# Three rounds between a split and its output products: a re-timed software pipeline on one TensorE

## Chip, cores and metric

The kernel runs on one NeuronCore of a Trainium2 chip. The metric is the device time of one execution in microseconds (us). PE is TensorE (matmuls), PEld its weight loads, DVE VectorE, ACT ScalarE, POOL GpSimd, SP the engine whose queue issues the DMAs.

## What is computed

```python
X = np.fft.fft(np.fft.fft(x, axis=1), axis=2).real     # x is (8, 3072, 256)
x = X.reshape(8 * 3072, 256)
h = x @ w_in                                           # (256, 2048)
x = (h - np.tanh(h)) @ w_out                           # (2048, 256)
h = x @ w_in2                                          # (256, 1024)
sm = softmax(h); solu = h * sm
ln = (solu - mean(solu)) / sqrt(var(solu) + 1e-6) * g_ln
out = ln @ w_out2                                      # (1024, 256)
```

All of it is float32. The kernel keeps the accuracy by writing each float32 operand as a high and a low part and adding the products high x high, high x low, low x high (`PASSES`).

## The kernel before, in words

A first stage of some 190 us makes the Fourier transform with the symmetry of a real input, so that only half of the columns are computed, and converts the weights. What follows, about 3450 us, is one loop over **rounds** (`step` in the code, 768 of them): 48 groups `n` of 512 tokens, 16 blocks `m` of 128 hidden units. In a round TensorE makes the hidden block `h` (line 879: `parity` for the block before, then `even` for this one, six products of 256 columns), then adds an older block's share to the 512 tokens' second-layer input `x2p` (`o1`, line 941, six products of 512 columns). VectorE combines the block (`act_in`, line 904), subtracts the tanh (`act_out`, line 921) and prepares the next block (`lead`, line 897); ScalarE takes the tanh (line 912) and the high part of the result; GpSimd takes the low part (line 169, called from `rest`). For two of eight blocks VectorE takes the low part instead (`low_by_vector`).

The second layer (`layer2`) is laid over these rounds in a fixed order written by hand. Two tiles of 128 tokens make a **pair**; a pair comes every eight rounds, and each of its works stands at so many rounds behind the pair's start ("back" in the lists `ahead`, `early` and `late`, which say where in a round the work is put into the engines' queues: before the loop's own VectorE preparation, before `o1`, or after it). I count the eight rounds of the cycle from 0 to 7, so that back 17 is position 1. Each engine works through its own queue in order; a semaphore holds an instruction until what it reads is written and what it overwrites has been read.

For a pair, `product` (line 970) makes seven products with the second hidden matrix in two PSUM banks, `bank_a` and `bank_b` (Strassen's scheme in Winograd's form: the first product also goes, by a ScalarE copy, line 1114, into the other bank; `kept`, line 985, copies a finished half out, `block`, line 992, combines halves on VectorE and takes the maximum). Then come the exponential (`power`, ScalarE), the weighing with it (`weigh`, VectorE, line 1016), the square sum (`square`), three small GpSimd steps for the norm (`scale`), and the transposition (`turn`): VectorE transposes 32x32 blocks (line 1046), one DMA writes them to DRAM and four read them back into `um`, with the tokens moved to the free dimension (line 1052). `split_moved` takes the high part of half a tile on ScalarE and the low part on GpSimd, into `ut`, a ring of two buffers. `outp` multiplies each half with the last weights: four times a product of 512 columns with the high part (line 1074) and one of 256 columns with the low part (line 1081), all into one tile `po`. `scaled` brings `po` out: ScalarE scales one half into `o` (line 1092), VectorE adds the other (line 1093), SP stores it.

Before, the cycle's second half reads: splits at backs 14, 16, 18, 20; output products at 15, 17, 19, 21; `scaled` at 18 and 22, in the list ahead of everything else that VectorE does for the second layer. There is one PSUM bank for `po`, `p_t`, with one buffer: a tile's first output product waits until the tile before it is scaled and added. The other seven banks hold `x2p` (two), `bank_a`, `bank_b` and `h` (three).

Of the kernel before, what the change touches and what calls it, by code (L numbers as in the profile page):

```python
# [10 lines left out]
F32 = mybir.dt.float32  # L11
# [3 lines left out]
AF = mybir.ActivationFunctionType  # L15
ALU = mybir.AluOpType
# [4 lines left out]
B, S, D = 8, 3072, 256  # L21
FF1, FF2 = 2048, 1024
P = 128
# [116 lines left out]
def fft2_moe_moe_kernel(  # L140
    ctx: ExitStack, tc: tile.TileContext, xr, x8, xn, xn8, w_in, w_out, w_in2, w_out2, g_ln, tt, t8, ft, out
):
    nc = tc.nc
# [556 lines left out]
    for q in range(NQ):  # L700
# [28 lines left out]
        if q == NQ - 4:  # L729
            nc.sync.dma_start(out=wnu, in_=wnu_d.rearrange("o (m p) -> p (o m)", p=P))  # L730
            nc.sync.dma_start(
                out=nu_h, in_=nu_d[:, PAIRS : PAIRS + 1].rearrange("b o -> o b").to_broadcast([P, B])
# [22 lines left out]
    wk = pool(ctx, "wk", 2, side="left")  # L755
# [15 lines left out]
    B11, B21, B22, T1, T2, T3, T4 = range(7)  # L771
# [3 lines left out]
    A11, A12, A21, A22, S1, S4, S2, S3 = range(8)  # L775
# [92 lines left out]
    bank_a = p_pr.tile([P, HF], F32, tag="a", name="bank_a")  # L868
# [96 lines left out]
    h2s, es, us, sts, uts, pts, pos, o2s, moved = {}, {}, {}, {}, {}, {}, {}, {}, {}  # L965

    def product(p, bank, a, b, start=False):

        for q, (hx, hw) in enumerate(PASSES):
            nc.tensor.matmul(  # L970
                in_pairs(bank),
                xs[:, hx, xs_at[a]],
                in_turn(wi2[:, b, hw]),
                start=(start and q == 0),
                stop=(q == 2),
                skip_group_check=True,
            )

    def new_u(t):
        us[t] = (wk.tile([P, FF2], F32, tag="u", bufs=3, name=f"u{t}"), None)  # L980
        sts[t] = wk.tile([P, 12], F32, tag="st", bufs=8, name=f"st{t}")
        return us[t][0]

    def kept(t, f):
        nc.scalar.copy(out=us[t][0][:, f * HF : (f + 1) * HF], in_=bank_b)
# [3 lines left out]
    def block(t, f, bank, other, first):  # L989

        u, st = us[t][0][:, f * HF : (f + 1) * HF], sts[t]
        nc.vector.tensor_tensor_reduce(  # L992
            out=u,
            in0=bank,
            in1=u if other else nothing_more.to_broadcast([P, HF]),
            scale=-1.0,
            scalar=FLOOR if first else st[:, 7:8],
            op0=ALU.add,
            op1=ALU.min,
            accum_out=st[:, 7:8] if first else st[:, 0:1],  # L1000
        )
# [20 lines left out]
    def square(t):  # L1022

        u, e = us[t]
        st = sts[t]
        nc.scalar.activation(out=st[:, 3:4], in_=st[:, 2:3], func=AF.Copy, scale=-1.0 / (32 * FF2))
        nc.scalar.activation(  # L1027
            out=e, in_=u, func=AF.Square, scale=1.0 / 32, bias=st[:, 3:4], accum_out=st[:, 6:7]
        )

    def scale(t):

        st = sts[t]
        g = nc.gpsimd
        g.tensor_scalar(
            out=st[:, 4:5], in0=st[:, 1:2], scalar1=1e-9, scalar2=1e-3, op0=ALU.add, op1=ALU.mult
        )
        g.tensor_scalar(  # L1038
            out=st[:, 5:6], in0=st[:, 4:5], scalar1=st[:, 4:5], scalar2=st[:, 6:7], op0=ALU.mult, op1=ALU.add
        )  # L1040
        g.tensor_tensor(out=st[:, 10:11], in0=st[:, 5:6], in1=mhalf, op=ALU.pow)  # L1041

    def turn(t):
        u = us[t][0]
        tb = mv.tile([P, FF2], F32, tag="t", bufs=1, name=f"tb{t}")
        nc.vector.transpose(out=tb, in_=u)  # L1046
        d = mv_d[t % len(mv_d)]
        nc.sync.dma_start(out=d, in_=tb)
        m = mv.tile([P, FF2], F32, tag="m", name=f"um{t}")
        blocks = d.rearrange("(q p) (k a j) -> a p k q j", q=4, a=4, j=32)  # L1050
        for a in range(4):
            nc.sync.dma_start(
                out=m[32 * a : 32 * a + 32].rearrange("p (k q j) -> p k q j", q=4, j=32), in_=blocks[a]
            )
        moved[t] = m

    def split_moved(t, half):
        m = moved[t][:, half * 512 : (half + 1) * 512]
        ut = wk.tile([P, 2, 512], F32R, tag="ut", bufs=2, name=f"ut{t}_{half}")
        rnd(ut[:, 0], m)  # L1060
        rest(nc.gpsimd, ut[:, 1], m, ut[:, 0])
        uts[t, half] = ut
        if half:
            moved.pop(t)

    def outp(t, half):
        if half == 0:
            pos[t] = taken(bank_o, [P, 512], "t", f"po{t}")
        po = pos[t]
        ut = uts.pop((t, half))  # L1070
        for k4 in range(4):
            k = half * 4 + k4
            ks = slice(k4 * P, (k4 + 1) * P)
            nc.tensor.matmul(  # L1074
                in_pairs(po),
                ut[:, 0, ks],
                wo2[:, k].rearrange("p h x n -> p (x n) h"),
                start=(k == 0),
                stop=False,
            )  # L1080
            nc.tensor.matmul(  # L1081
                in_pairs(po[:, :D]),
                ut[:, 1, ks],
                wo2[:, k, :, 0].rearrange("p h n -> p n h"),
                start=False,
                stop=(k == NK2 - 1),
            )

    def scaled(t):
        po, by = pos.pop(t), sts.pop(t)[:, 10:11]  # L1090
        o = wk.tile([P, D], F32, tag="o", bufs=3, name=f"o{t}")
        nc.scalar.activation(out=o, in_=po[:, D:], func=AF.Copy, scale=by)  # L1092
        nc.vector.scalar_tensor_tensor(
            out=o, in0=po[:, :D], scalar=by, in1=o, op0=ALU.mult, op1=ALU.add
        )
        us.pop(t)
        nc.sync.dma_start(out=out[t * P : (t + 1) * P, :], in_=o)
# [8 lines left out]
    def layer2(step, place):  # L1106

        works = {
            "ahead": (
                (0, lambda p: product(p, bank_a, A11, B11, True)),  # L1110
                (2, lambda p: product(p, bank_a, A12, B21)),
                (4, lambda p: product(p, bank_b, S3, T3)),
                (6, lambda p: product(p, bank_b, A22, T4)),
                (1, lambda p: nc.scalar.copy(out=bank_b, in_=bank_a)),
                (3, lambda p: (new_u(2 * p), kept(2 * p, 1))),
                (5, lambda p: (new_u(2 * p + 1), kept(2 * p + 1, 1))),
            ),
            "early": (
                (15, lambda p: outp(2 * p + 1, 0)),
                (17, lambda p: outp(2 * p + 1, 1)),  # L1120
                (19, lambda p: outp(2 * p, 0)),
                (21, lambda p: outp(2 * p, 1)),
                (18, lambda p: scaled(2 * p + 1)),
                (22, lambda p: scaled(2 * p)),
                (3, lambda p: block(2 * p, 0, bank_a, False, True)),
                (5, lambda p: block(2 * p + 1, 1, bank_a, True, True)),
                (6, lambda p: block(2 * p + 1, 0, bank_b, False, False)),
                (7, lambda p: block(2 * p, 1, bank_a, True, False)),
                (7, lambda p: power(2 * p + 1)),
                (8, lambda p: (power(2 * p), weigh(2 * p + 1))),  # L1130
                (9, lambda p: weigh(2 * p)),
                (10, lambda p: (square(2 * p + 1), scale(2 * p + 1), turn(2 * p + 1))),
                (12, lambda p: (square(2 * p), scale(2 * p), turn(2 * p))),
                (14, lambda p: split_moved(2 * p + 1, 0)),
                (16, lambda p: split_moved(2 * p + 1, 1)),
                (18, lambda p: split_moved(2 * p, 0)),
                (20, lambda p: split_moved(2 * p, 1)),
                (-1, lambda p: split_x2(p, A11, A12)),
                (1, lambda p: split_x2(p, S2, S3)),
                (3, lambda p: split_x2(p, A22, S4)),  # L1140
            ),
            "late": (
                (2, lambda p: product(p, bank_b, S2, T2)),
                (4, lambda p: product(p, bank_a, S1, T1, True)),
                (6, lambda p: product(p, bank_a, S4, B22)),
            ),
        }
        for back, work in works[place]:
            p = pair_at(step, back)
            if p is not None:  # L1150
                work(p)
# [92 lines left out]


    base = 4 * NG - 8
    block(base + 2, 1, bank_a, True, False)
    first.close()
    p_o = pool(ctx, "p_o", 2, space=PSUM)
    p_h2 = pool(ctx, "p_h2", 2, space=PSUM)  # L1250
# [77 lines left out]
    def exponent(t):  # L1328
        power(t, h2s.get(t))

    def weighed(t):
        weigh(t, h2s.pop(t, None))

    works = {
        "T": trans, "r": high, "l": low_of, "H": h2, "W": outp, "w": last_outp, "X": x_high, "x": x_low,
        "m": peak, "e": exponent, "u": weighed, "q": square, "c": scale, "o": scaled, "M": split_moved,
        "z": last_store,
    }
    todo = """X4 x4 e3 W10 M11 X5 H40 x5 e2 M00 u3 W11 o1 M01 H41 W00 m4 T30 e4 u2 W01 o0 r30 H50 T31 l30 X6 r31 q3 c3 x6
# [55 lines left out]
```

## Time and profile before

| | |
|---|---|
| runs | 3709.53, 3725.9, 3733.6 us; median 3725.9 |
| profiled execution | 3713.57 us, span 3711.8 us from first to last instruction |
| busy share | TensorE 84%, weight loads 70%, VectorE 62%, ScalarE 55%, GpSimd 53% |
| clock of TensorE granted on the mean | 0.913 of 2.4 GHz |

A matmul's busy time is modelled and overlaps with its neighbour's, so the distance between the starts of two groups of matmuls is the better measure. "Idle before" and the waits name what released the instruction. A half granted clock (0.5) is 1.2 GHz.

### The profile page before, as it was taken

How to read it: one execution, taken by the hardware profiler on the slowest of the kernel's cores; microseconds unless marked ns; L12 is line 12 of the kernel's file. 1: busy time of each engine (PE TensorE's matmuls, PEld its weight loads, DVE VectorE, ACT ScalarE, POOL GpSimd, SP SyncE). 2: the span in 40 equal slices, each digit the busy share in tenths (PEclk: the TensorE clock that was granted, in tenths of full speed). 3: DMA queues.
4: the chain of work that ended last, by engine and by line, in shares of the span. 5: the costliest groups of instructions: out<-in, count | busy, mean ns of one | idle time of the engine just before them, and what ended most of it. 6: DMA issues, size and time to landing. Idle time of an engine off the chain costs nothing.

```text
span 3711.8 us, 47081 instructions
## 1 busy us (share of the span) xinstructions
PE 3107.8 (84%) x15073; PEld 2607.3 (70%) x15073; DVE 2300.3 (62%) x4577; ACT 2046.2 (55%) x3990; POOL 1966.5 (53%) x2121
## 2 busy tenths in 40 slices
PE   9998888888888888888888888888888888888888
PEld 5777677776677767776777677767776776677766
DVE  9975665556656565656566665565565566656665
ACT  4565555555555555555555555555555555555555
POOL 0275555555555555555555555555555555555553
PEclk9999998889888998988999988998898999889999
DMA  9813232323232323232333322332232323232322
GB/s 359 304 39 72 64 77 69 69 67 74 63 74 62 77 66 74 69 73 66 72 69 73 74 63 69 73 74 63 69 73 66 71 68 73 67 70 69 73 64 53
DMA packets 882648, 302.96 MB, mean 82 GB/s; under 512 B 788544, under 2 KB 844144, under 8 KB 879104
## 3 DMA queue, kind: packets, MB, share of 16 engines
q1 hardware_dynamic: 879792, 293.45, 31.9%
q10 hardware_dynamic: 2304, 6.42, 0.4%
q8 instruction: 120, 1.97, 0.2%
q14 instruction: 128, 1.05, 0.1%
q0 software_dynamic: 304, 0.07, 0.0%
HBM read 161.26 MB, written 138.60 MB: 81 GB/s over the span
## 4 chain that ended last, share of the span: by engine, by line
PE 39%; POOL 18%; ACT 15%; issue 12%; DVE 11%; DMA 3%; SPq 1%; ACTq 0%; POOLq 0%; DVEq 0%
PE x2p L941 17%; POOL ut L169 10%; PE po L1074 9%; PE po L1081 7%; PE h L879 5%; ACT t L912 5%; DVE h L904 4%; POOL gh L169 4%; ACT gh L166 4%; ACT e L1027 4%; ACT o L1092 2%; DMA um<-mv_d 2%; DVE u L992 2%; POOL st L1038 2%; POOL st L1041 2%
## 5 line engine op out<-in xcount | busy, mean ns | idle before, releaser
L169 POOL TENSOR_TENSOR gh<-t,gh 128x512 fp32r<-128x512 f32 x584 | 877.1, 1502 | 898.4 <-ACT gh L166 536.1
L941 PE MATMUL x2p<-gh,wo 128*128 128x512 f32 x4608 | 1304.3, 426 | 0.0
L912 ACT ACTIVATE t<-h 128x512 f32<-128x512 f32 x762 | 454.3, 596 | 1535.5 <-DVE h L904 1252.2
L941 PEld LDWEIGHTS x2p<-gh,wo 128*128 128x128 f32 x4608 | 977.0, 220 | 166.4 <-POOL gh L169 0.4
L904 DVE SCALAR_TENSOR_TENSOR h<-asb,h 128x256 f32<-128x256 f32 x762 | 322.5, 423 | 1169.1 <-PE h L879 1168.0
L1081 PE MATMUL po<-wo,ut 128*128 128x256 f32 x1528 | 518.1, 339 | 403.6 <-POOL ut L169 403.6
L169 POOL TENSOR_TENSOR ut<-um,ut 128x512 fp32r<-128x512 f32 x372 | 506.4, 1361 | 536.9 <-ACT ut L166 536.9
L1074 PE MATMUL po<-wo,ut 128*128 128x512 f32 x1528 | 671.0, 461 | 107.4 <-ACT ut L166 97.3
L879 PEld LDWEIGHTS h<-zs,wt 128*128 128x128 f32 x4572 | 656.7, 196 | 141.0 <-PE h L879 84.1
L879 PE MATMUL h<-zs,wt 128*128 128x256 f32 x4572 | 667.7, 279 | 72.9 <-DVE gh L169 70.6
L1081 PEld LDWEIGHTS po<-wo,ut 128*128 128x128 f32 x1528 | 343.9, 225 | 486.2 <-POOL ut L169 486.1
L1074 PEld LDWEIGHTS po<-wo,ut 128*128 128x128 f32 x1528 | 332.2, 217 | 197.2 <-ACT ut L166 159.4
L921 DVE TENSOR_TENSOR t<-h,t 128x512 f32<-128x512 f32 x578 | 394.6, 683 | 0.0
L166 ACT ACTIVATE gh<-t 128x512 fp32r<-128x512 f32 x584 | 367.8, 630 | 3.4 <-DVE t L921 1.9
L897 DVE SCALAR_TENSOR_TENSOR asb<-nb,wnu,h 128x256 f32<-128x256 f32 x762 | 358.6, 471 | 0.0
L1016 DVE SCALAR_TENSOR_TENSOR u<-u,e 128x1024 f32<-128x1024 f32 x188 | 330.0, 1755 | 0.0
L970 PE MATMUL bank_a<-wi,xs 128*128 128x512 f32 x1128 | 306.3, 380 | 2.4 <-POOL xs L169 1.5
L169 POOL TENSOR_TENSOR xs<-xb,xs 128x256 fp32r<-128x256 f32 (+1 forms) x282 | 231.6, 821 | 57.7 <-ACT xs L166 53.7
L1046 DVE STREAM_TRANSPOSE tb<-u 128x1024 f32<-128x1024 f32 x186 | 230.0, 1237 | 0.0
L970 PE MATMUL bank_b<-wi,xs 128*128 128x512 f32 x846 | 229.7, 380 | 0.2 <-POOL xs L169 0.2
L166 ACT ACTIVATE ut<-um 128x512 fp32r<-128x512 f32 x372 | 229.8, 618 | 0.0
L1027 ACT ACTIVATE e<-u,st 128x1024 f32<-128x1024 f32 x192 | 221.5, 1154 | 6.2
(156 smaller groups left out, 3018.1 us busy)
## 6 DMA issues: line engine op xcount, KB each, us to landing
mv_d<-tb SPq DMA_DIRECT2D x186, 512.0 KB, 2.6
um<-mv_d SPq DMA_DIRECT2D x744, 128.0 KB, 3.7
out<-o SPq DMA_DIRECT2D x192, 128.0 KB, 1.7
x<-xr SPq DMA_DIRECT2D x23, 1024.0 KB, 10.8
zf<-z_d SPq DMA_DIRECT2D x64, 128.0 KB, 2.5
z_d<-zt ACTq DMA_DIRECT2D x16, 392.0 KB, 6.5
wi<-w_in SPq DMA_DIRECT2D x6, 1024.0 KB, 9.4
z_d<-zt SPq DMA_DIRECT2D x16, 384.0 KB, 10.1
```

What stands on the lines that cost most here:

```text
L166: nc.scalar.activation(out=o, in_=i, func=AF.Copy)
L169: eng.tensor_tensor(out=o, in0=i, in1=hi.bitcast(F32), op=ALU.subtract)
L879: nc.tensor.matmul(in_pairs(hs[n, m][:, 0]), wt[c][:, hw, u, o : o + P], in_turn(zs[:, hz, u]), start=(u == 0 and i == 0), stop=(i == 2), ...
L897: nc.vector.scalar_tensor_tensor(out=asb, in0=zg[n][1], scalar=wnu[:, m : m + 1], in1=hs[n, m][:, 0], op0=ALU.mult, op1=ALU.add)
L904: nc.vector.scalar_tensor_tensor(out=h[:, 1], in0=as_.pop((n, m)), scalar=2.0, in1=h[:, 0], op0=ALU.mult, op1=ALU.subtract)
L912: nc.scalar.activation(out=t, in_=h, func=AF.Tanh)
L921: nc.vector.tensor_tensor(out=g, in0=h, in1=t, op=ALU.subtract)
L941: nc.tensor.matmul(in_pairs(x2p[n][mt]), wo1[c][:, hw, k, mt * P : (mt + 1) * P], in_turn(gh[:, hg]), start=(m == 0 and i == 0), stop=(m = ...
L970: nc.tensor.matmul(in_pairs(bank), xs[:, hx, xs_at[a]], in_turn(wi2[:, b, hw]), start=(start and q == 0), stop=(q == 2), skip_group_check= ...
L1027: nc.scalar.activation(out=e, in_=u, func=AF.Square, scale=1.0 / 32, bias=st[:, 3:4], accum_out=st[:, 6:7])
L1074: nc.tensor.matmul(in_pairs(po), ut[:, 0, ks], wo2[:, k].rearrange("p h x n -> p (x n) h"), start=(k == 0), stop=False,)
L1081: nc.tensor.matmul(in_pairs(po[:, :D]), ut[:, 1, ks], wo2[:, k, :, 0].rearrange("p h n -> p n h"), start=False, stop=(k == NK2 - 1),)
```

## The change

Output products stand three rounds behind their split (backs 17, 19, 21, 23 for splits at 14, 16, 18, 20). `scaled` keeps only ScalarE's part, put at the end of the rounds of the second halves (backs 19 and 23); VectorE's addition and the store become `store`, a round later (20 and 24), and stand in the list behind `weigh` and `turn`. The first product of a pair, A11 x B11, moves from the front of position 0 to its end, behind `o1`. The copy of a half for the pair's second tile (`new_u`, `kept` for `2p + 1`, in the title U3's copy) moves from the front of position 5 to the end of position 4. One output half that falls behind the last round, and its `scaled` and `store`, are added after the loop.

```diff
     def scaled(t):
-        po, by = pos.pop(t), sts.pop(t)[:, 10:11]
-        o = wk.tile([P, D], F32, tag="o", bufs=3, name=f"o{t}")
-        nc.scalar.activation(out=o, in_=po[:, D:], func=AF.Copy, scale=by)
+        o = o2s[t] = wk.tile([P, D], F32, tag="o", bufs=3, name=f"o{t}")
+        nc.scalar.activation(out=o, in_=pos[t][:, D:], func=AF.Copy, scale=sts[t][:, 10:11])
+
+    def store(t):
+        o = o2s.pop(t)
         nc.vector.scalar_tensor_tensor(
-            out=o, in0=po[:, :D], scalar=by, in1=o, op0=ALU.mult, op1=ALU.add
+            out=o, in0=pos.pop(t)[:, :D], scalar=sts.pop(t)[:, 10:11], in1=o, op0=ALU.mult, op1=ALU.add
         )
         us.pop(t)
         nc.sync.dma_start(out=out[t * P : (t + 1) * P, :], in_=o)
...
             "ahead": (
-                (0, lambda p: product(p, bank_a, A11, B11, True)),
...
-                (5, lambda p: (new_u(2 * p + 1), kept(2 * p + 1, 1))),
             ),
             "early": (
-                (15, lambda p: outp(2 * p + 1, 0)),
-                (17, lambda p: outp(2 * p + 1, 1)),
-                (19, lambda p: outp(2 * p, 0)),
-                (21, lambda p: outp(2 * p, 1)),
-                (18, lambda p: scaled(2 * p + 1)),
-                (22, lambda p: scaled(2 * p)),
+                (17, lambda p: outp(2 * p + 1, 0)),
+                (19, lambda p: outp(2 * p + 1, 1)),
+                (21, lambda p: outp(2 * p, 0)),
+                (23, lambda p: outp(2 * p, 1)),
...
                 (12, lambda p: (square(2 * p), scale(2 * p), turn(2 * p))),
+                (20, lambda p: store(2 * p + 1)),
+                (24, lambda p: store(2 * p)),
...
             "late": (
+                (0, lambda p: product(p, bank_a, A11, B11, True)),
                 (2, lambda p: product(p, bank_b, S2, T2)),
                 (4, lambda p: product(p, bank_a, S1, T1, True)),
                 (6, lambda p: product(p, bank_a, S4, B22)),
+                (4, lambda p: (new_u(2 * p + 1), kept(2 * p + 1, 1))),
+                (19, lambda p: scaled(2 * p + 1)),
+                (23, lambda p: scaled(2 * p)),
             ),
...
     base = 4 * NG - 8
+    outp(base - 2, 1)
     block(base + 2, 1, bank_a, True, False)
+    scaled(base - 2)
+    store(base - 2)
```

## Rows read from the trace of the kernel before

**Rows 1.** Page, part 1: busy us (share of the span) xinstructions by engine

```profile
PE 3107.8 (84%) x15073; PEld 2607.3 (70%) x15073; DVE 2300.3 (62%) x4577; ACT 2046.2 (55%) x3990; POOL 1966.5 (53%) x2121
```

**Rows 2.** Waits, whole span: engine line <- releaser: us, times, longest

```profile
PEld po L1081 <- POOL ut L169: 486.1, 278, 1.9
...
PEld po L1074 <- ACT ut L166: 159.4, 276, 1.5
...
PEld h L879 <- PE h L879: 84.1, 91, 1.1
...
DVE u L992 <- ACT u L985: 74.8, 94, 1.9
```

**Rows 3.** Timeline of TensorE, positions 7, 0, 1, 2, 3: start, us, instruction

```profile
1816.14 0.57 PE L879 MATMUL h<-zs,wt 128*128 128x256 f32 x3 [0.74 <-DVE gh L169]
1816.55 0.38 PE L1074 MATMUL po<-wo,ut 128*128 128x512 f32 x1
...
1817.86 1.46 PE L941 MATMUL x2p<-gh,wo 128*128 128x512 f32 x6
1819.15 0.83 PE L879 MATMUL h<-zs,wt 128*128 128x256 f32 x6
1819.82 0.81 PE L970 MATMUL bank_a<-wi,xs 128*128 128x512 f32 x3
1820.47 1.46 PE L941 MATMUL x2p<-gh,wo 128*128 128x512 f32 x6
1821.77 0.83 PE L879 MATMUL h<-zs,wt 128*128 128x256 f32 x6
1823.08 0.48 PE L1074 MATMUL po<-wo,ut 128*128 128x512 f32 x1 [0.48 <-ACT ut L166]
1825.16 0.38 PE L1081 MATMUL po<-wo,ut 128*128 128x256 f32 x1 [1.60 <-POOL ut L169]
...
1827.66 0.83 PE L879 MATMUL h<-zs,wt 128*128 128x256 f32 x6
...
1830.92 0.83 PE L879 MATMUL h<-zs,wt 128*128 128x256 f32 x6
```

**Rows 4.** Cores: span and granted clock on the mean

```profile
core 0: 3711.8 us, clock 0.913
```

**Rows 5.** One line over the span: min/median/max ns, first and last start

```profile
L1016 DVE SCALAR_TENSOR_TENSOR u<-u,e x188: 1209/1619/2314, 234.1 to 3670.3; 128x1024 f32<-128x1024 f32 x188
```

**Rows 6.** Windows: length, busy (instructions) PE, PEld, DVE, ACT, POOL, clock, DMA, GB/s

```profile
1825.16:1830.92 5.76, 5.75 (x32) 5.20 (x32) 3.70 (x9) 3.44 (x8) 3.85 (x3) 1.00 0.00 0
...
1834.05:1838.22 4.17, 4.17 (x14) 3.46 (x15) 0.37 (x1) 0.31 (x1) 2.47 (x5) 0.59 0.42 68
1811.64:1886.06 74.42, 62.10 (x314) 53.01 (x313) 45.77 (x91) 42.45 (x83) 40.77 (x44) 0.93 0.32 73
```

**Rows 7.** Timeline of VectorE, positions 0 to 2 of the cycle of rows 3

```profile
1821.68 2.30 DVE L1016 SCALAR_TENSOR_TENSOR u<-u,e 128x1024 f32<-128x1024 f32 x1
...
1823.92 0.42 DVE L904 SCALAR_TENSOR_TENSOR h<-asb,h 128x256 f32<-128x256 f32 x1
...
1828.19 0.43 DVE L904 SCALAR_TENSOR_TENSOR h<-asb,h 128x256 f32<-128x256 f32 x1 [1.39 <-PE h L879]
```

**Rows 8.** Timeline of VectorE, position 0 of the next cycle

```profile
1856.71 0.43 DVE L904 SCALAR_TENSOR_TENSOR h<-asb,h 128x256 f32<-128x256 f32 x1 [1.71 <-PE h L879]
...
1858.04 1.37 DVE L1016 SCALAR_TENSOR_TENSOR u<-u,e 128x1024 f32<-128x1024 f32 x1
```

**Rows 9.** VectorE's output addition over the span

```profile
L1093 DVE SCALAR_TENSOR_TENSOR o<-po,st,o x191: 483/484/486, 270.8 to 3707.4; 128x256 f32<-128x256 f32 x191
```

**Rows 10.** Timeline of GpSimd, position 0 of the cycle of rows 3

```profile
1821.51 1.40 POOL L169 TENSOR_TENSOR gh<-t,gh 128x512 fp32r<-128x512 f32 x1 [1.60 <-issue]
```

**Rows 11.** Reads of the transposed tile: landing, from issue

```profile
DMA to landing us min/median/max: 2.8/3.7/5.1
```

**Rows 12.** Timeline of SP after the transposition of position 2

```profile
1831.94 0.32 SPq L1048 DMA_DIRECT2D mv_d<-tb  x1
1834.90 3.77 SPq L1052 DMA_DIRECT2D um<-mv_d  x4
```

More of the change, by code (lines that the diff above doesn't have):

```diff
@@ L1329, in exponent, with stored @@
         power(t, h2s.get(t))
+    def stored(t):
+        scaled(t)
+        store(t)
     def weighed(t):
@@ L1335, in fft2_moe_moe_kernel @@
         "T": trans, "r": high, "l": low_of, "H": h2, "W": outp, "w": last_outp, "X": x_high, "x": x_low,
-        "m": peak, "e": exponent, "u": weighed, "q": square, "c": scale, "o": scaled, "M": split_moved,
+        "m": peak, "e": exponent, "u": weighed, "q": square, "c": scale, "o": stored, "M": split_moved,
         "z": last_store,
```

## The prediction

> **What bounds the kernel now.** The page comes first: TensorE is the fullest engine, VectorE, ScalarE and GpSimd are between 53 and 62% busy [rows 1]. So the question is what TensorE waits for. The list of waits answers it: its weight loads stood 486.1 us for GpSimd's low part of `ut`, 159.4 us for ScalarE's high part of it, and 84.1 us at `h` [rows 2]. The first two are the output products, which stand one round behind their split. The timeline of TensorE then shows where: in an odd round the first output product waits 0.48 us for the high part, the next 1.60 us for the low part [rows 3], while the even rounds run without a gap.
>
> From the same timeline comes what a pair costs TensorE without waits at full clock [rows 3]: six products of `h` take 0.67 us (1819.15 to 1819.82), a product of the second layer 0.65 (to 1820.47), `o1` 1.30 (to 1821.77), four output products of each kind 1.31 (1816.55 to 1817.86). Position 0 is 2.62 us, positions 2, 4, 6 are 3.26 (1827.66 to 1830.92), an odd position 0.67 + 1.31 + 1.30 = 3.28. The cycle of eight: 2.62 + 3 x 3.26 + 4 x 3.28 = **25.5 us**.
>
> What it takes now: the 188 `weigh` start between 234.1 and 3670.3 us [rows 5], which is 93 cycles and one round of some 4 us, so **36.9 us** a cycle (two cycles in one window: 74.42 [rows 6]). The difference is accounted for. Output products run in about 92 cycles; (486.1 + 159.4 + 84.1)/92 = 7.9 us are waits. The granted clock of 0.913 [rows 4] means 8.7% of the span's work lost, 323 us or 3.5 us a cycle. 25.5 + 7.9 + 3.5 = 36.9. The clock falls behind those waits: from 1825 to 1831 it was 1.00 with TensorE busy throughout, from 1834 to 1838, right after another wait for a split, 0.59 [rows 6], between the levels 2.4 and 1.2 GHz. So nothing but these waits and the clock stands between 36.9 and 25.5; the most that can be gained is 11.4 x 92 = 1049 us.
>
> **The change, part by part.** *Output products three rounds later.* The low part is ready about 1.6 us after TensorE wants it in the next round [rows 3]; two further rounds of over 3 us put it some 5 us ahead. This removes 486.1 + 159.4 us, 7.0 a cycle. The work itself stays the same. The ring of `ut` has two buffers, so ScalarE's split of position 2 now waits for the output products of position 1, one round back instead of three: ScalarE comes to it some 3.5 us into its round, the products end before that round begins. No cost; if the cover were gone, ScalarE's queue (the next tanh) would stand behind it.
>
> *`scaled` split in two.* VectorE no longer stands in positions 2 and 6 for ScalarE's half, and the addition (0.48 us [rows 9]) leaves position 6. There it had delayed the low part behind it, for which TensorE stood 0.74 us in position 7 [rows 3], 84.1 us in all. I let that go to zero: without the addition the low part ends about 3.2 us into a round of 3.26, and TensorE needs it 0.33 later.
>
> *The bank of `po`: the new wait.* The next tile's first output product may start only when the addition has read the one bank. In position 4 the addition ends 0.53 + 1.33 + 1.24 (transposition) + 0.48 = 3.6 us after the round's start, TensorE wants the bank at 3.26 + 0.67 = 3.9: covered by 0.3 us. In position 0 it is not, for the addition stands behind `weigh`. VectorE's first step follows TensorE's round by 0.53 us (1827.66 to 1828.19 [rows 3, 7]). In one cycle `weigh` starts 2.53 us into the round and the next instruction could start at 4.77 (1823.92 - 1819.15 [rows 3, 7]); with the addition 5.25. TensorE wants the bank at 2.62 + 0.67 = 3.29: it waits **2.0 us**. In the next cycle, where no sum of the second layer's inputs lies ahead of it, `weigh` starts 1.86 us into the round (1858.04 less 1856.71, plus 0.53) and ends at 3.2 [rows 8]: with the addition 3.7, a wait of **0.4 us**; there the copy for the next group moves closer in ScalarE's and GpSimd's queue, so I take 0.8. Both cycles alternate. Behind the added wait of TensorE stands its whole queue, `o1` and the next `h`, and behind the later VectorE its `act_in` of position 1.
>
> *First product to the end of position 0.* Same work, 0.65 us; the copy of position 1 stands behind ScalarE's tanh, which needs a later product of TensorE anyway, so it costs nothing. `o1` comes 0.65 us earlier in that round; GpSimd's low part of the block is used by its last two products, 0.9 us after the first, so it stays covered. *U3's copy to position 4.* ScalarE has it half a round earlier, and VectorE's wait of 74.8 us [rows 2] goes; off the path, nothing gained. ScalarE's positions 4 and 3 get 0.6 and 0.5 us fuller, 3.7 and 2.7 of 3.3.
>
> *SP.* The stores move behind the five DMAs of a transposition; `o` has three buffers, so the next writer comes a cycle and a half later. The transposed tile is the tighter one. Position 2's transposition ends 3.1 us into its round, the write takes 3.0 until SP goes on to the reads and these 3.8 to issue [rows 12], and a read lands 2.8 to 5.1 us after its issue [rows 11]: 12.7 to 15.0 us. ScalarE splits it in position 6, at 13.0 + 2.1 = 15.1. Covered, by 0.1 at worst; before, with longer rounds, by far more.
>
> *Other engines.* Two cycles hold 45.8 us of VectorE, 42.5 of ScalarE, 40.8 of GpSimd [rows 6]: 22.9, 21.2 and 20.4 in a cycle of 27 to 28. None becomes the bound by its sum, but VectorE is at 83%.
>
> *The clock.* The trace of before shows no long wait that stands alone, so I bound it. Now 3.5 us a cycle are lost behind three waits of about 2 us (positions 1, 3 and 5; the 0.74 us of position 7 are followed by full clock), 1.2 us each. A lone wait of 2.0 us costs between 0 and that; I take 1.2, since it is the same wait at the same place, and 0 in the cycle with 0.8 us.
>
> **The sum.** One cycle 25.5 + 2.0 + 1.2 = 28.7, the next 25.5 + 0.8 = 26.3, mean **27.5**. 36.9 - 27.5 = 9.4 us, in 92 cycles 865 us. The loop's end gets eight matmuls and one addition outside, some 2 us. 3713.6 - 865 + 2 = **2850 us**, against a profiled execution that lies 0.3% under the median of the runs shown (3725.9); I keep 2850.
>
> **Rivals.** *A, GpSimd first everywhere.* `weigh` took 1209 to 2314 ns [rows 5]. In the long case GpSimd had begun a low part 0.17 us before it and took 1.40 us [rows 7, 10], so VectorE stood about 1.1 us; in the short case `weigh` was first. With rounds shifted against each other GpSimd may be first in every position 0: a wait of 1.5 to 2.0 us in both cycles, with the lower clock behind both: 25.5 + 1.9 + 1.2 = 28.6 and over, 92 x 1.1 = 100 us more, 2950. For it: GpSimd's copy work moves closer to that place. Against it: the order was the same in all cycles of before.
> The Trainium skill (SBUF — State Buffer, section "SBUF: two separate sides") has a rule for this pair: a VectorE instruction with two SBUF inputs and a GpSimd instruction lock a shared pair of ports, whoever starts first holds it to its end and the other blocks. The durations above agree with it, and by it the output addition, with one input in PSUM, isn't held, as its 483 to 486 ns show [rows 9].
>
> *B, the in-order queues.* Long odd rounds let the three other engines catch up; without them a small lateness can come back to TensorE, as at position 7 now (0.74 us), or a late transposed tile can hold ScalarE's split and the tanh behind it. If four of eight rounds lost 0.74, the cycle would be 30.5 us, 3125; all eight, 33.4 and 3390. Against: I followed each engine's queue through a cycle of 27.5 us, and found no other wait; for: margins of 0.1 to 0.5 us.
>
> *C, the bank's ring makes it slower.* One bank goes from first product to addition twice in a cycle. Now that takes three rounds of four, then all four. If ScalarE's half or the addition slipped behind two further rounds at each tile, the ring would be 6 rounds, the cycle 12 rounds of 3.26, 39.1 us: 92 x 2.2 = 200 us slower, 3915. It decides from 18.5 us a ring (37/2); the rows give 12.4 to 14.5.
>
> *D, it doesn't do what it says:* if the output products still waited for a split (a late tile read), 36 to 37 us a cycle, within 1% of before.
>
> **How the numbers follow.** Forecast (2770 to 2920): 0.65. A (2920 to 2990): 0.12. B (2990 to 3450): 0.13. Better than 2770 (no loss of clock, short waits): 0.05. D 0.02, C 0.03. The range of 8 in 10 takes the forecast, A and the near part of B: 2770 to 3060. A per cent is about what a measurement here can tell from none. Faster by over 1%: 0.95; within 1%: 0.02; slower: 0.03.
>
> **What would show it.** Right: the waits for `ut` gone from TensorE; in their place waits of the first output product for VectorE's addition, about 92, half of them near 2 us; rounds of 2.6 to 3.3 us elsewhere; a granted clock of 0.97 or more; VectorE over 75% busy. Wrong: TensorE waiting for `gh`, `h` or `xs` in many rounds, ScalarE idle at `ut` for the read, or a clock still near 0.91 with shorter waits.

## The result, and the profile after

The changed kernel takes **2815.0 us** (median of four runs, 2809.4 to 2820.3) where the kernel before takes 3725.6: a ratio of **0.756**, 95% interval 0.753 to 0.7589. The forecast was 2850, with 2770 to 3060. The profiled execution took 2820.3 us.

Part 1 of the page after, and its chain of work that ended last (share of the span by engine):

```profile
PE 2698.5 (96%) x15073; PEld 2380.6 (84%) x15073; DVE 2258.5 (80%) x4577; ACT 2029.2 (72%) x3990; POOL 1980.9 (70%) x2121
...
PE 82%; DVE 11%; issue 4%; DMA 1%; ACT 1%; POOL 0%; SPq 0%; DVEq 0%; POOLq 0%; ACTq 0%
```

The busy time of the three other engines is what it was to within 2% [rows 1], in a span 24% shorter; TensorE's fell by 13% for the same instructions, since fewer of them run at half clock. The chain ends on TensorE, with VectorE as the only other engine of weight. The granted clock and `weigh` over the span:

```profile
core 0: 2818.5 us, clock 0.984
```

```profile
L1016 DVE SCALAR_TENSOR_TENSOR u<-u,e x188: 1209/1291/2347, 241.5 to 2777.0; 128x1024 f32<-128x1024 f32 x188
```

From the first to the last `weigh` it is 93 cycles and a round of some 4 us, as before [rows 5]: (2777.0 - 241.5 - 4)/93 = **27.2 us** a cycle, 27.5 were forecast, 36.9 it had been. Between the first and the last `weigh` that saves 901 us (3436.2 to 2535.5); the first one starts 7 us later than before, and 893 us are left, by which the profiled executions differ.

The waits of TensorE after, of the whole list, which has the first stage in it too, those over 8 us:

```profile
PEld po L1074 <- DVE o L1095: 113.3, 94, 2.2
...
PEld x2p L941 <- POOL gh L169: 15.0, 51, 1.0
...
PEld h L879 <- DVE asb L897: 8.4, 12, 2.4
```

The two waits for `ut` and the one at `h` [rows 2] are gone, 730 us; one has come, 94 times, for VectorE's addition into `o` (now line 1095), that is, for the one bank of `po`. Cycles come in two kinds by turns: in a long one two sums of the second layer's inputs (line 957) lie ahead of `weigh` in position 0, in a short one they do not. The timeline of TensorE shows where the wait is; positions 7, 0, 1 and 2 of a long cycle (start, us, instruction):

```profile
1518.16 1.46 PE L941 MATMUL x2p<-gh,wo 128*128 128x512 f32 x6
1519.46 0.83 PE L879 MATMUL h<-zs,wt 128*128 128x256 f32 x6
1520.12 1.46 PE L941 MATMUL x2p<-gh,wo 128*128 128x512 f32 x6
1521.42 0.81 PE L970 MATMUL bank_a<-wi,xs 128*128 128x512 f32 x3
1522.07 0.83 PE L879 MATMUL h<-zs,wt 128*128 128x256 f32 x6
1524.75 0.48 PE L1074 MATMUL po<-wo,ut 128*128 128x512 f32 x1 [1.85 <-DVE o L1095]
...
1526.16 1.46 PE L941 MATMUL x2p<-gh,wo 128*128 128x512 f32 x6
1527.46 0.83 PE L879 MATMUL h<-zs,wt 128*128 128x256 f32 x6
```

Position 7 no longer has its gap [rows 3]. In position 1 the first output product starts 2.68 us into the round (1522.07 to 1524.75) where 0.67 would do: 2.0 us. VectorE in the same place:

```profile
1521.32 0.75 DVE L957 TENSOR_TENSOR xb<-xb 128x256 f32<-128x256 f32 x2
1521.99 2.30 DVE L1016 SCALAR_TENSOR_TENSOR u<-u,e 128x1024 f32<-128x1024 f32 x1
...
1524.22 0.47 DVE L1095 SCALAR_TENSOR_TENSOR o<-po,st,o 128x256 f32<-128x256 f32 x1
1524.62 0.41 DVE L904 SCALAR_TENSOR_TENSOR h<-asb,h 128x256 f32<-128x256 f32 x1
```

and GpSimd, whose low part starts 0.18 us before `weigh`:

```profile
1521.81 1.40 POOL L169 TENSOR_TENSOR gh<-t,gh 128x512 fp32r<-128x512 f32 x1 [1.09 <-PE x2p L941]
```

`weigh` takes 2.30 us behind it, as it did before [rows 7, 10], and the addition stands behind `weigh`. The rounds of position 1 in four long cycles one after the other, as windows (length, busy by engine, granted clock, DMA), and the wait in the second of them:

```profile
1412.92:1418.31 5.39, 3.54 (x21) 3.08 (x20) 5.39 (x10) 3.31 (x7) 4.25 (x3) 1.00 0.07 24
1466.57:1473.64 7.07, 5.22 (x22) 4.32 (x21) 5.42 (x10) 3.31 (x7) 5.92 (x4) 0.76 0.05 19
1522.07:1527.46 5.39, 3.54 (x21) 3.08 (x20) 5.39 (x10) 3.31 (x7) 4.25 (x3) 1.00 0.07 24
1575.72:1582.80 7.08, 5.23 (x22) 4.32 (x21) 5.43 (x10) 3.32 (x7) 5.94 (x4) 0.76 0.06 20
```

```profile
1469.25 0.48 PE L1074 MATMUL po<-wo,ut 128*128 128x512 f32 x1 [1.85 <-DVE o L1095]
```

The wait is the same in all four. In the second and the fourth the clock then falls, and the round takes 1.7 us longer. Over the whole trace the clock falls behind 21 of the 44 waits of some 2 us, and behind none of the shorter ones: 21 x 1.7 = 36 us. So the new wait costs twice, the second time in about half of the long cycles.

### The profile page after: what moved, and what is told of

It is laid out like the page before. It is cut to its first block, busy times and chain, and to the rows that moved or that the text cites. A ratio compares the mean times of both kernels' runs of the same rounds, so it can differ in the third digit from the quotient of the medians.

```text
span 2818.5 us, 47312 instructions
## 1 busy us (share of the span) xinstructions
PE 2698.5 (96%) x15073; PEld 2380.6 (84%) x15073; DVE 2258.5 (80%) x4577; ACT 2029.2 (72%) x3990; POOL 1980.9 (70%) x2121
## 4 chain that ended last, share of the span: by engine, by line
PE 82%; DVE 11%; issue 4%; DMA 1%; ACT 1%; POOL 0%; SPq 0%; DVEq 0%; POOLq 0%; ACTq 0%
PE x2p L941 31%; PE h L879 15%; PE po L1074 13%; PE bank_b L970 7%; PE bank_a L970 6%; PE po L1081 6%; DVE u L1016 4%; DVE asb L897 2%; PE pz L486 1%; DVE h L904 1%; DVE o L1095 1%; PE pz L505 1%; DVE xb L957 1%; DVE t L921 1%; PE pw L397 1%
## 5 line engine op out<-in xcount | busy, mean ns | idle before, releaser
L941 PE MATMUL x2p<-gh,wo 128*128 128x512 f32 x4608 | 1148.8, 386 | 1.4 <-POOL gh L169 1.4
L169 POOL TENSOR_TENSOR gh<-t,gh 128x512 fp32r<-128x512 f32 x584 | 809.3, 1386 | 383.7 <-ACT gh L166 257.5
L941 PEld LDWEIGHTS x2p<-gh,wo 128*128 128x128 f32 x4608 | 846.2, 193 | 126.3 <-POOL gh L169 15.0
L169 POOL TENSOR_TENSOR ut<-um,ut 128x512 fp32r<-128x512 f32 x372 | 546.3, 1469 | 182.4 <-PE x2p L941 136.0
L879 PE MATMUL h<-zs,wt 128*128 128x256 f32 x4572 | 638.4, 276 | 6.0 <-DVE asb L897 4.7
L1074 PE MATMUL po<-wo,ut 128*128 128x512 f32 x1528 | 546.9, 397 | 95.8 <-DVE o L1095 94.8
L1081 PE MATMUL po<-wo,ut 128*128 128x256 f32 x1528 | 425.6, 279 | 0.0
L1074 PEld LDWEIGHTS po<-wo,ut 128*128 128x128 f32 x1528 | 295.4, 193 | 146.8 <-DVE o L1095 113.3
L1081 PEld LDWEIGHTS po<-wo,ut 128*128 128x128 f32 x1528 | 300.0, 196 | 0.2
L1016 DVE SCALAR_TENSOR_TENSOR u<-u,e 128x1024 f32<-128x1024 f32 x188 | 295.7, 1573 | 0.0
L970 PEld LDWEIGHTS bank_a<-wi,xs 128*128 128x128 f32 x1128 | 206.2, 189 | 25.4 <-POOL xs L169 0.2
```

The costliest lines, as they stand in the source:

```text
L169: eng.tensor_tensor(out=o, in0=i, in1=hi.bitcast(F32), op=ALU.subtract)
L879: nc.tensor.matmul(in_pairs(hs[n, m][:, 0]), wt[c][:, hw, u, o : o + P], in_turn(zs[:, hz, u]), start=(u == 0 and i == 0), stop=(i == 2), ...
L941: nc.tensor.matmul(in_pairs(x2p[n][mt]), wo1[c][:, hw, k, mt * P : (mt + 1) * P], in_turn(gh[:, hg]), start=(m == 0 and i == 0), stop=(m = ...
L970: nc.tensor.matmul(in_pairs(bank), xs[:, hx, xs_at[a]], in_turn(wi2[:, b, hw]), start=(start and q == 0), stop=(q == 2), skip_group_check= ...
L1016: nc.vector.scalar_tensor_tensor(out=u, in0=u if h is None else h, scalar=-1.0 if h is None else 1.0, in1=e, op0=ALU.mult, op1=ALU.mult, a ...
L1074: nc.tensor.matmul(in_pairs(po), ut[:, 0, ks], wo2[:, k].rearrange("p h x n -> p (x n) h"), start=(k == 0), stop=False,)
```

## The experiments

Each kernel is the changed one with the edit shown, unless it says otherwise. All were run in groups beside the kernel before (medians 3721 to 3727 us). The cycle times are from the first and last `weigh`, as above.

**One round again.**

```diff
-                (17, lambda p: outp(2 * p + 1, 0)),
-                (19, lambda p: outp(2 * p + 1, 1)),
-                (21, lambda p: outp(2 * p, 0)),
-                (23, lambda p: outp(2 * p, 1)),
+                (15, lambda p: outp(2 * p + 1, 0)),
+                (17, lambda p: outp(2 * p + 1, 1)),
+                (19, lambda p: outp(2 * p, 0)),
+                (21, lambda p: outp(2 * p, 1)),
...
-                (20, lambda p: store(2 * p + 1)),
-                (24, lambda p: store(2 * p)),
+                (18, lambda p: store(2 * p + 1)),
+                (22, lambda p: store(2 * p)),
...
-                (19, lambda p: scaled(2 * p + 1)),
-                (23, lambda p: scaled(2 * p)),
+                (17, lambda p: scaled(2 * p + 1)),
+                (21, lambda p: scaled(2 * p)),
...
-    outp(base - 2, 1)
     block(base + 2, 1, bank_a, True, False)
-    scaled(base - 2)
-    store(base - 2)
```

> The change with the distance alone undone: output products one round behind their split again (15, 17, 19, 21), ScalarE's part at the end of rounds 17 and 21, VectorE's addition at 18 and 22; the list order, the first product and U3's copy stay as changed. Theory (the waits for the split are the whole gain): TensorE stands again about 7 us a cycle for ut and loses about 3.5 us to the clock, only the 0.74 us at position 7 stay away, so 25.5 + 7.0 + 3.5 = 36.0 us a cycle and about 3640 us. Rival (the gain comes from a lighter VectorE list and the moved product): under 3100 us, with the waits for ut shorter than half of before.

Measured: 3661.0 us, ratio 0.9835 (0.9804 to 0.9866), clock 0.912, 36.1 us a cycle. Its waits:

```profile
PEld po L1081 <- POOL ut L169: 521.8, 278, 2.2
...
PEld po L1074 <- ACT ut L166: 126.4, 276, 1.5
...
PEld h L879 <- PE h L879: 5.6, 16, 0.4
```

The distance alone undone, 846 of the 911 us are gone again, with the waits for `ut` and the clock of before. What is left, 1.7%, fits the low part of position 6 that the addition no longer delays: TensorE's wait at `h` is 5.6 us where it was 84.1 [rows 2].

**Distance alone.** The kernel before with only the distance changed.

```diff
-                (15, lambda p: outp(2 * p + 1, 0)),
-                (17, lambda p: outp(2 * p + 1, 1)),
-                (19, lambda p: outp(2 * p, 0)),
-                (21, lambda p: outp(2 * p, 1)),
-                (18, lambda p: scaled(2 * p + 1)),
-                (22, lambda p: scaled(2 * p)),
+                (17, lambda p: outp(2 * p + 1, 0)),
+                (19, lambda p: outp(2 * p + 1, 1)),
+                (21, lambda p: outp(2 * p, 0)),
+                (23, lambda p: outp(2 * p, 1)),
+                (20, lambda p: scaled(2 * p + 1)),
+                (24, lambda p: scaled(2 * p)),
...
+    outp(base - 2, 1)
     block(base + 2, 1, bank_a, True, False)
+    scaled(base - 2)
```

> The kernel before with the distance alone: output products at 17, 19, 21, 23, the undivided scaling (ScalarE's half, VectorE's addition, store) at 20 and 24 where it stood in the list, ahead of weigh and turn; product and copy not moved. Theory: the waits for ut go; VectorE stands about 0.7 us for ScalarE's half in positions 0 and 4, but the bank is free 3.1 us into position 0, before TensorE wants it at 3.3, so that wait goes too; instead lead of position 1 is late by 0.5 to 1 us in one cycle of two: 26 to 27 us a cycle, 2700 to 2790 us. Rival (the division of scaled is needed): VectorE's stand for ScalarE comes through to TensorE in both positions, 28 to 29 us a cycle, 2870 to 2960 us.

Measured: **2741.1 us**, ratio 0.7366 (0.7343 to 0.7388), clock 0.998, 26.4 us a cycle. The theory holds: less of the change does more. Its position 0 on VectorE, a long cycle:

```profile
1533.51 0.76 DVE L957 TENSOR_TENSOR xb<-xb 128x256 f32<-128x256 f32 x2
1534.26 0.49 DVE L1093 SCALAR_TENSOR_TENSOR o<-po,st,o 128x256 f32<-128x256 f32 x1
1534.66 1.83 DVE L1016 SCALAR_TENSOR_TENSOR u<-u,e 128x1024 f32<-128x1024 f32 x1
```

The addition stands ahead of `weigh`, the bank is free in time. What TensorE waits for in the loop instead is, above all, `lead` and, at the first product in front of position 0, GpSimd's low part of `xs`, the split input of the second layer:

```profile
PEld h L879 <- DVE asb L897: 44.2, 101, 4.8
PEld bank_a L970 <- POOL xs L169: 42.5, 94, 1.9
```

So the other three edits together cost 74 us against this kernel. The next three runs say which.

**Additions first.** Only their place in VectorE's list.

```diff
                 (23, lambda p: outp(2 * p, 1)),
+                (20, lambda p: store(2 * p + 1)),
+                (24, lambda p: store(2 * p)),
                 (3, lambda p: block(2 * p, 0, bank_a, False, True)),
...
                 (12, lambda p: (square(2 * p), scale(2 * p), turn(2 * p))),
-                (20, lambda p: store(2 * p + 1)),
-                (24, lambda p: store(2 * p)),
```

> The changed kernel with VectorE's additions listed ahead of weigh (position 0) and turn (position 4) instead of behind. Theory (the new wait at position 1 is the one bank, read late behind weigh): the bank is free 2.4 to 3.0 us into position 0, TensorE wants it at 3.3, the waits of the first output product go from about 95 us to under 10; VectorE's position 0 ends as late as it does now, so TensorE stands about 0.8 us at position 2 for lead in one cycle of two; the clock is at 1.00; 25.9 us a cycle, 2690 us. Rival 1 (VectorE's position 0 is what bounds, not the bank): the wait moves to lead in full, 2800 to 2820 us. Rival 2 (weigh, pushed 0.45 us later, finds GpSimd's low part begun in both cycles and stands behind it): 2720 to 2760 us, with a shortest weigh near 2 us at position 0.

Measured: **2723.8 us**, ratio 0.7322 (0.7302 to 0.7342), clock 1.000, 26.2 us a cycle: faster than both kernels, 91 us under the changed one. What TensorE still waits for in the loop:

```profile
PEld x2p L941 <- POOL gh L169: 58.5, 97, 1.6
PEld h L879 <- DVE asb L897: 37.3, 58, 2.4
```

The wait for the bank is off the list, as the theory said. The time, though, is not the theory's 2690 but in the range of rival 2. Of the rest, 37 us are the wait for `lead` that was expected, 58 us, which were not, are for GpSimd's low part in `o1`. Rival 2 is right in part: in position 0 `weigh` now stands behind GpSimd in both cycles, but for less than it said, 1.60 us in the short cycle and 1.91 in the long one (1.29 and 2.30 on the median in the changed kernel). And in position 1 of the long cycle the second `weigh` holds off GpSimd's low part, which starts 0.1 us behind it and takes 2.26 us for its 1.28:

```profile
1493.40 1.60 DVE L1016 SCALAR_TENSOR_TENSOR u<-u,e 128x1024 f32<-128x1024 f32 x1
...
1520.11 1.91 DVE L1016 SCALAR_TENSOR_TENSOR u<-u,e 128x1024 f32<-128x1024 f32 x1
...
1523.61 1.21 DVE L1016 SCALAR_TENSOR_TENSOR u<-u,e 128x1024 f32<-128x1024 f32 x1
```

```profile
1523.71 2.26 POOL L169 TENSOR_TENSOR gh<-t,gh 128x512 fp32r<-128x512 f32 x1 [0.54 <-ACT gh L166]
```

**First product at the front again.**

```diff
             "ahead": (
+                (0, lambda p: product(p, bank_a, A11, B11, True)),
...
             "late": (
-                (0, lambda p: product(p, bank_a, A11, B11, True)),
```

> The changed kernel with the first product A11 x B11 at the front of position 0 again. Theory: no difference, 2805 to 2825 us, for what it might wait there TensorE would wait in position 1 for the bank anyway. Rival: GpSimd's low part of its input lands 1.3 us into the round, the product wants it at 1.1 or earlier, TensorE stands 0.3 us a cycle for it and this comes through: 2840 us.

Measured: 2781.1 us, ratio 0.7475 (0.7455 to 0.7494), clock 0.999. Neither: 34 us *faster*. TensorE's positions 0 and 1 in a long cycle:

```profile
1548.74 0.83 PE L879 MATMUL h<-zs,wt 128*128 128x256 f32 x6
1549.41 1.13 PE L970 MATMUL bank_a<-wi,xs 128*128 128x512 f32 x3
1550.38 1.46 PE L941 MATMUL x2p<-gh,wo 128*128 128x512 f32 x6
1551.67 0.83 PE L879 MATMUL h<-zs,wt 128*128 128x256 f32 x6
1554.04 0.48 PE L1074 MATMUL po<-wo,ut 128*128 128x512 f32 x1 [1.54 <-DVE o L1095]
...
1556.75 0.83 PE L879 MATMUL h<-zs,wt 128*128 128x256 f32 x6
```

From position 0 to position 2 it is 8.01 us (1548.74 to 1556.75), in the changed kernel at full clock 8.00 (1519.46 to 1527.46). The wait is as long, but it comes in two stretches, 0.3 us in front of the first product's third part and 1.7 for the bank. The long cycles are alike in this, and the clock falls behind none of them: 0.999 against 0.984, 1.5% of some 2800 us, 42 us of work.

```profile
PEld po L1074 <- DVE o L1095: 79.4, 48, 1.8
```

The theory's sentence on waits was right, its time wrong, for it had left out the clock.

**U3's copy back.**

```diff
             "ahead": (
...
+                (5, lambda p: (new_u(2 * p + 1), kept(2 * p + 1, 1))),
...
             "late": (
...
-                (4, lambda p: (new_u(2 * p + 1), kept(2 * p + 1, 1))),
```

> The changed kernel with U3's copy at the front of position 5 again. Theory: no difference, 2800 to 2830 us: VectorE stands some 0.8 us for it in position 5 and has the time. Rival: this comes back to TensorE as a wait for lead or low part in position 6 or 7, over 2840 us.

Measured: 2809.2 us, ratio 0.7533 (0.7515 to 0.7551): no difference from 0.756 (0.753 to 0.7589).

**First product at the front, additions first.** Both edits above together.

> The additions ahead of weigh and turn, and the first product at the front of position 0 again. With the product at the front the changed kernel gained 34 us. Theory (that gain was clock alone: the same wait cut in two stretches, 0.3 and 1.6 us, no longer let the clock fall): here the clock is at 1.00 anyway, so nothing is gained, the wait of 0.3 us for the product's input appears and the ones behind it shrink: 2720 to 2745 us. Rival (the front is the better place by itself): about 2690 us.

Measured: 2726.1 us, ratio 0.7314 (0.73 to 0.7328), clock 1.000, against 2723.8 without the front place. Where the clock stands at full speed already, the place of the first product is worth nothing. Together with the front place's own run, and with the 36 us counted above, this shows that the 34 us were the clock's.

**The sums a round later, and a round earlier.** Four kernels after one question: does the long wait hang on who starts first, `weigh` or GpSimd?

```diff
-            for blk in {3: (S1,), 4: (S2, S3), 5: (S4,)}.get(j, ()):
+            for blk in {3: (S1,), 5: (S2, S3, S4)}.get(j, ()):
```

and for the sums earlier

```diff
-            for blk in {3: (S1,), 4: (S2, S3), 5: (S4,)}.get(j, ()):
+            for blk in {3: (S1, S2, S3), 5: (S4,)}.get(j, ()):
```

> The changed kernel with the two sums that VectorE makes in position 0 of every other cycle made a round later, ahead of the third. Theory (who comes first, weigh or GpSimd's low part, decides the long wait for the bank): weigh starts 1.9 us into position 0 in both cycles, ahead of the low part at 2.35, takes about 1.3 us instead of 2.3, the first output product waits 0.3 us instead of 2.0, the clock stays at 1.00; the long cycle goes from 28.4 to about 26.2 us, 2710 us in all. Rival 1 (weigh is slow there for another reason): it still takes 2.3 us, waits of 1.3 us, 2780 us or more. Rival 2 (the work only moves to position 1): the low part of position 1 or lead is late by 0.8 us and more, 2750 to 2780 us.

> The additions ahead of weigh and turn, and the two sums a round later. Theory: with both waits for the bank gone the rest is GpSimd's low part and VectorE's lead in positions 1 and 2; 26.1 us in both cycles, 2705 to 2720 us, a little under the kernel with the additions first alone (2724). Rival (the sums push the second weigh behind GpSimd's low part): 2730 to 2745 us.

> The changed kernel with the two sums of position 0 made a round earlier, in position 7, where VectorE has 0.9 us to spare and GpSimd's low part begins only 0.5 us after them. Theory (weigh held by GpSimd's low part makes the long wait, and the sums a round later failed only because GpSimd then held the sums): weigh starts first in every position 0 and takes 1.2 to 1.3 us, the first output product waits 0.3 us in every cycle, the sums take 0.4 us each, the clock stays at 1.00; the long cycle goes from 28.4 to 26.1 us, 2710 us. Rival (VectorE is simply full between positions 7 and 1): the block of position 7 or act_in of position 0 is late and TensorE waits for lead, 2740 to 2780 us.

> The additions ahead of weigh and turn, and the two sums a round earlier. Theory: no wait for the bank, both cycles like the short one of the kernel with the additions first (26.0 us, with TensorE held 0.5 us in position 2 by GpSimd's low part): 2695 to 2715 us, the shortest of all. Rival (the second weigh then meets GpSimd's low part and gives it back): 2720 to 2735 us, no better than the additions first alone (2724).

| kernel | us | ratio, interval | us a cycle |
|---|---|---|---|
| changed, sums later | 2751.5 | 0.7378 (0.7359 to 0.7397) | 26.5 |
| changed, sums earlier | 2763.7 | 0.742 (0.7395 to 0.7445) | 26.6 |
| additions first, sums later | 2764.3 | 0.7418 (0.7403 to 0.7433) | 26.7 |
| additions first, sums earlier | 2779.2 | 0.7466 (0.7444 to 0.7489) | 26.8 |

On the changed kernel the mechanism is as expected and the time is not. VectorE with the sums later, positions 0 and 1 of the cycle that was long:

```profile
1540.81 1.22 DVE L1016 SCALAR_TENSOR_TENSOR u<-u,e 128x1024 f32<-128x1024 f32 x1
...
1541.95 0.48 DVE L1095 SCALAR_TENSOR_TENSOR o<-po,st,o 128x256 f32<-128x256 f32 x1
...
1543.67 2.78 DVE L957 TENSOR_TENSOR xb<-xb 128x256 f32<-128x256 f32 x3
```

`weigh` now comes first and takes 1.22 us for 2.30. But the three sums, 0.41 each when alone (the two in position 0 take 0.75 together in the changed kernel), take 2.78 us, for two of them stand behind GpSimd, one behind the low part of `ut`, one behind that of the block (shortest, median and longest in ns, and GpSimd):

```profile
L957 DVE TENSOR_TENSOR xb<-xb x3: 414/1029/1494, 1543.7 to 1546.0; 128x256 f32<-128x256 f32 x3
```

```profile
1543.13 1.28 POOL L169 TENSOR_TENSOR ut<-um,ut 128x512 fp32r<-128x512 f32 x1
1544.38 1.45 POOL L169 TENSOR_TENSOR gh<-t,gh 128x512 fp32r<-128x512 f32 x1
```

TensorE's wait for the bank falls from 113.3 us over the trace to 35.4, and in its place it waits 35.7 us for `lead` and 11.3 for `xs`. A round earlier the third of the sums is held, 1.51 us, and TensorE waits 42.9 us for `lead` and still 56.7 for the bank:

```profile
L957 DVE TENSOR_TENSOR xb<-xb x3: 419/425/1507, 1546.3 to 1547.1; 128x256 f32<-128x256 f32 x3
```

```profile
1546.33 2.30 DVE L957 TENSOR_TENSOR xb<-xb 128x256 f32<-128x256 f32 x3
```

```profile
1546.83 1.52 POOL L169 TENSOR_TENSOR gh<-t,gh 128x512 fp32r<-128x512 f32 x1 [1.54 <-ACT gh L166]
```

Both times lie where the rival expected them that has TensorE wait for `lead` instead (rival 2 of the sums later), yet both kernels are faster than the changed one, by 64 and 51 us. On the kernel with the additions first, where the bank had cost nothing any more, both moves only lose, 40 and 55 us; their expectations, theory and rival, had counted the sums at 0.4 us and missed this. In position 0 the sums lie ahead of GpSimd's low part, and for that kernel it is the better place for them.

## Why the prediction came out, point by point

*The gain.* Right, and for the reason given. The waits for `ut` went to nothing. One round again brings 846 of 911 us back, and the distance alone gives more than the whole change. The cycle was forecast at 27.5 us and is 27.2. By its terms: the bank took 1.2 us a cycle for 1.4, the clock 0.4 for 0.6, and 0.2 to 0.3 are other waits that had been put at nothing, which offsets a part of the rest.

*The ring of `ut`, the later reads, the queues (rival B).* The covers held. No wait for `ut`'s buffers is on the list, ScalarE's waits for the transposed tile sum to 0.3 us, and at every position but 1 and 2 the median round takes its 2.6 to 3.3 us. Rival B is out for the changed kernel: its 15 and 8 us for GpSimd and `lead` are at most 0.3 us a cycle.

*The bank of `po`.* Right in place and size for the long cycle: 2.0 us forecast, 2.0 measured. In the short one 0.8 were taken, with 0.4 worked out from the rows; 113.3 us in 94 waits are 1.2 on the mean, so the short one is 0.4. I had guessed that ScalarE's and GpSimd's copies, moved closer, would lengthen `weigh` there; they don't. That the bank was the cause, and not VectorE's fill, is shown by the additions first.

*The clock.* The granted 0.984 leaves 1.6% of 2818.5 us, 45 us, over the whole span. In the loop 36 us of it are the 21 falls behind the long wait, 0.8 for each of 44 long waits, where 1.2 were taken. It is no cost of every wait: a lone wait of 2.0 us costs 1.7 us of clock in about half of the long cycles and nothing in the others.

*First product, "it costs nothing".* Wrong, though hidden in the total: the step counted waits only. In front, it cut TensorE's stand in two; at the end, the whole 2.0 us stand in one piece, and that costs 34 us of clock. *U3's copy:* nothing gained, as said.

*The split of `scaled`.* I charged the new wait to the one bank and took the place behind `weigh` as given. With the same addition ahead of `weigh` the wait is gone and 91 us with it. The split itself is worth little: additions first, which has it, beat the distance alone by 17 us (0.7322 against 0.7366, intervals that just part). With the first product in front as well, so that only the split and U3's copy differ from the distance alone, it is 15 us (0.7314).

*Rival A.* Its mechanism is real, its case did not arise. GpSimd is first in every second position 0, as before. Putting `weigh` first shortens it from 2.30 to 1.22 us. The rule of the Trainium skill (SBUF — State Buffer, section "SBUF: two separate sides"), by which, of a VectorE instruction with two SBUF inputs and a GpSimd instruction that reads SBUF, the one that starts later is blocked until the other ends, agrees with this, with the sums' 2.30 and 2.78 us, and with the addition, whose one input lies in PSUM: 440 to 485 ns in all of 191.

*What stays open.* The best kernel still has 26.2 us a cycle against 25.5 without waits. Its two waits, at the start of position 2 and in its `o1`, follow the rounds in which VectorE and GpSimd hold each other off; no order tried removes both, and whether one exists is not shown. What decides in which of the long cycles the clock falls was not tried, nor whether it stays up in the divided wait because the wait is divided or because its longest piece is shorter. Of distances only one and three rounds were tried.

## To carry to other kernels

When the fullest engine waits for a split made one round earlier, put the consumer further behind, as far as the ring of buffers covers it (here three rounds), and then look for what is held longer because of it: here the one PSUM bank, whose last reader should stand first in its engine's queue. Of a wait, count the pieces too: the same 2 us in one piece can cost the clock that they leave alone in two.

## What the runs showed of the hardware that was not expected

- The same stand of TensorE, 2.0 us between positions 0 and 2, left the granted clock at 0.999 when cut into 0.3 and 1.7 us and lowered it to 0.984 in one piece: it fell behind 21 of 44 such waits, for 1.7 us each.
- Three VectorE sums of 0.41 us take 2.30 to 2.78 us when GpSimd's low parts come between them: in the longer case one sum took 1.03 us behind one low part and the next 1.49 behind another, where one long instruction that started first (`weigh`, 1.22 us) passes.
